# Second linear layer's q inside the second pass, grad_out by tiles, weight flips elsewhere, dWo of the last layer from on-chip o

## The chip, the cores and the metric

The kernel runs on one core of a Trainium2 chip. The time is that of one execution on the device in microseconds (us); the figure compared is the median over several runs. Times inside an execution come from one profiled execution.

## The reference

Four layers on x [1, 2048, 640] in bf16 with 32 heads of 20, alternating linear attention (A) and sliding-window attention of 256 (B), and the whole backward pass:

```python
def _A_ref(x, wqkv, wo):
    ...
    phi = lambda t: jnp.where(t > 0, t + 1, jnp.exp(t)) + 1e-6
    pq, pk = phi(q), phi(k)
    kv = jnp.einsum("bhsd,bhse->bhde", pk, v)
    z = jnp.einsum("bhsd->bhd", pk)
    num = jnp.einsum("bhqd,bhde->bhqe", pq, kv)
    den = jnp.einsum("bhqd,bhd->bhq", pq, z)[..., None] + 1e-6
    o = num / den
    ...
# _B_ref: softmax(q k^T / sqrt(20)) over the last 256 positions, times v
x = A_x
x = x + _A_ref(_layernorm(x, axis=-1), A_wqkv, A_wo)
x = x + _B_ref(_layernorm(x, axis=-1), B_wqkv, B_wo)
x = x + _A_ref(_layernorm(x, axis=-1), A_wqkv, A_wo)
x = x + _B_ref(_layernorm(x, axis=-1), B_wqkv, B_wo)
# returned: x and, from grad_out, the gradients of A_x, A_wqkv, A_wo, B_wqkv, B_wo
```

## The kernel before

The layers are numbered 0 (A), 1 (B), 2 (A), 3 (B). The 2048 positions are 16 tiles of 128. A "flip" is a transpose done by DMA, always issued from SP (line 404); plain DMAs go through SP or ACT (line 400).

`forward` goes through the tiles in two passes. `ab_pass(0)` does for each tile the numerator and division of layer 0 (`a_num`; its matmuls are at lines 624 and 432), the output projection, LN and qkv of layer 1 (`out_proj`, `ln`, `b_qkv`), the sliding attention (`attn`: scores at line 764, exponentials at 768 and 771, values at 802) and its output projection, and, two tiles behind, LN, k and v of layer 2 (`a_first`). Layer 2's q is not computed there: its normed input stays, flipped, in pqT, in the place of the q to come. `ab_pass(2)` then does the same for layers 2 and 3, and beside it, by `dO_steps`, the gradient dO of layer 3's attention output (grad_out tile flipped, times Wo_B flipped), with the sums that the softmax gradient needs.

Between the passes stand `late_q` for all 16 tiles (q of layer 2: ten matmuls at line 534, exponential at 538, minimum at 540, sum at 542, flip back into pqT, stores of pq and eq), `a_kv(2)` (the kv sums over all tiles, mbd), and `early_dO` (grad_out loaded in two halves over pk, Wo_B flipped into WoTB).

Buffers are rings, used in the order of the program. Those that matter here: s1, two PSUM tiles for the fourth head of a score group, which late_q uses as well; mm, two PSUM tiles (mm_ps) through which all projections, numerators and dO go; e, four buffers e_sb for score exponentials; ee and pp for exponentials and q; wT, one buffer through which `wflips` turns 35 pieces of 160 KB of the weights for the backward pass (15 of Wqkv_B, 15 of Wqkv_A, 5 of Wo_A), flip in and store out, spread over the second pass; o3, two buffers for the o of layer 3, which is stored to DRAM. Many small buffers of the second pass lie over vv, the v of layer 2, which is dead after a_kv(2).

The order is written by a list planner (`Sched`): each piece of work has a place in the pass (`AT`: tile number plus an offset, in tiles), and from these and assumed durations and dependencies (with some that only keep order, such as `after_kv`) it fixes the order on each of the five queues. TensorE's work may run ahead of that order by at most AHEAD places; work marked filler is outside that limit. Hardware waits come from the buffers themselves. Each queue runs in its fixed order, so an instruction that waits holds up what follows.

After the forward pass, `bwd_phase(None, None, 3)` computes dWo of layer 3 (o transposed times grad_out, 160 matmuls at line 1014), loading o back column by column (om, from SP), with nine loads and flips of the first slabs for the attention backward in between (`attn_slabs`, lines 326 and 1440). Then `B_attn_bwd(3)` runs (first scores at line 1496), then the backward of layers 2 and 1 and 0, which the change does not touch.

## Time and profile before

| what | value |
|---|---|
| median of 3 runs | 2291.28 us (2289.39 to 2301.68) |
| profiled execution | 2304.79 us, span 2303.1 us |
| mean granted TensorE clock | 0.960 |
| TensorE, VectorE, ScalarE, GpSimd busy | 88%, 63%, 52%, 38% |
| DMA | 376.80 MB, mean 164 GB/s |
| first numerator, first score of the second pass | 454.62, 506.74 us |
| last projection of the forward pass, first scores of the attention backward | 759.28, 804.74 us |

The span runs from the first to the last instruction of the profiled execution; the execution's own time is 1.7 us longer. In what follows PE is TensorE, PEld its weight loads, DVE VectorE, ACT ScalarE, POOL GpSimd, SP SyncE; SPq and ACTq are DMA issues on these queues. The ends of matmuls are modelled by the profile.

### The profile page before, as it was taken

The numbers are of one execution on the slowest core, as the hardware profiler recorded it, in microseconds if no ns is written. First come the engines' busy times: TensorE is split into PE (matmuls) and PEld (weight loads), VectorE is DVE, ScalarE is ACT, GpSimd is POOL, SyncE is SP. The second block draws the span as 40 slices with busy tenths as digits, with TensorE's granted clock in tenths as the row PEclk, the third lists the DMA queues.
The fourth block names the chain that finished last, engine by engine and source line by source line (L and its number), as shares of the span: only waits on it lengthen the run. The fifth ranks groups of instructions, "written<-read, shape, count | busy, mean of one in ns | idle before, by whom it ended". The sixth has DMA issues, their size and how long they took to land. (4 is left out here: it accounts for less than half of the span.)

```text
span 2303.1 us, 68489 instructions
## 1 busy us (share of the span) xinstructions
PE 2030.2 (88%) x28066; PEld 1418.4 (62%) x28066; DVE 1454.3 (63%) x2994; ACT 1196.8 (52%) x1981; POOL 878.8 (38%) x1850
## 2 busy tenths in 40 slices
PE   6879998779998689999899989998999988997899
PEld 4646666546665367777656567656777775654664
DVE  6657776567675189999734349605989983443551
ACT  4527777327777188888522223215888871110330
POOL 1016666206777155555322213203555551220110
PEclk9979999899999789999999999998999999998999
DMA  7428887589998757776877789935767768878973
GB/s 257 163 97 182 177 188 174 172 216 214 216 221 190 166 108 135 124 132 128 174 163 162 183 167 207 184 100 126 126 132 124 134 138 170 189 161 195 194 152 101
DMA packets 944763, 376.80 MB, mean 164 GB/s; under 512 B 822720, under 2 KB 924736, under 8 KB 944192
## 3 DMA queue, kind: packets, MB, share of 16 engines
q1 hardware_dynamic: 862288, 295.75, 63.7%
q10 hardware_dynamic: 82160, 76.68, 10.9%
q8 instruction: 219, 3.59, 0.7%
q14 instruction: 96, 0.79, 0.1%
HBM read 111.64 MB, written 114.95 MB: 98 GB/s over the span
## 5 line engine op out<-in xcount | busy, mean ns | idle before, releaser
L1531 DVE TENSOR_TENSOR ds_sb<-pair,e_sb 128x768 bf16<-128x768 f32 x480 | 436.3, 948 | 45.1 <-POOL e_sb L1520 45.0
L1516 ACT ACTIVATE e_sb<-pair 128x768 bf16<-128x768 f32 x480 | 388.9, 812 | 113.4 <-PE pair L1496 107.7
L777 POOL TENSOR_SCALAR_AFFINE_SELECT e_sb<-e_sb 128x384 bf16<-128x384 bf16 (+1 forms) x512 | 197.8, 406 | 396.6 <-ACT e_sb L768 363.0
L768 ACT ACTIVATE e_sb<-s_ps 128x1152 bf16<-128x1152 f32 (+2 forms) x256 | 273.5, 1068 | 112.5 <-PE s_ps L764 71.3
L1014 PEld LDWEIGHTS <-om 128*128 128x128 bf16 x1920 | 193.7, 101 | 195.1 <-DMA om<-o 31.7
L1014 PE MATMUL mm_ps<-wq,dqT 128*128 128x320 bf16 x1920 | 283.7, 303 | 25.2 <-DMA dqT<-dqkv 25.1
L1523 POOL TENSOR_SCALAR_AFFINE_SELECT e_sb<-e_sb 128x256 bf16<-128x256 bf16 x448 | 182.1, 406 | 266.0 <-ACT e_sb L1516 257.4
L1014 PE MATMUL mm_ps<-dqkv,om 128*128 128x480 bf16 x1280 | 273.8, 373 | 0.0
L1185 POOL TENSOR_TENSOR gw<-w,gcar 128x640 f32<-128x640 f32 x64 | 89.4, 1397 | 483.0 <-ACT w L1182 473.5
L1520 POOL TENSOR_SCALAR_AFFINE_SELECT e_sb<-e_sb 128x256 bf16<-128x256 bf16 x512 | 206.5, 406 | 115.0 <-ACT e_sb L1516 113.6
L1014 PEld LDWEIGHTS <-dqT 128*128 128x128 bf16 x1920 | 185.1, 99 | 103.0 <-DMA dqT<-dqkv 29.3
L1167 ACT ACTIVATE dh<-mm_ps 128x320 f32<-128x320 f32 x128 | 56.0, 437 | 331.4 <-PE mm_ps L1014 289.6
L1544 PE MATMUL dsT_ps<-ident,ds_sb 128*128 128x128 bf16 x2244 | 193.4, 224 | 28.7 <-ACT dsT L1548 25.1
L1548 ACT COPY dsT<-dsT_ps 128x768 bf16<-128x768 bf16 x240 | 190.9, 795 | 12.4 <-PE dsT_ps L1544 6.4
L1544 PEld LDWEIGHTS <-ds_sb 128*128 128x128 bf16 x2244 | 140.3, 99 | 92.2 <-issue 88.7
L1560 PE MATMUL dqvk_ps<-Ksl,dsT 128*128 128x32 bf16 x2160 | 167.5, 178 | 3.8 <-DVE dqkv L1569 3.0
L1560 PEld LDWEIGHTS <-dsT 128*128 128x128 bf16 x2880 | 156.2, 97 | 22.8 <-issue 21.7
L432 PE MATMUL mm_ps<-Wqkv_B,hnTB 128*128 128x320 bf16 x960 | 166.3, 305 | 3.0 <-DVE qk_slab L673 1.6
L1564 PE MATMUL dqvk_ps<-dOsl,e_sb 128*128 128x32 bf16 x2160 | 165.2, 177 | 0.0
L1564 PE MATMUL dqvk_ps<-Qsl,ds_sb 128*128 128x32 bf16 x2160 | 165.2, 177 | 0.0
L1496 PE MATMUL pair<-KTg,QTg 32*128 32x384 bf16 (+2 forms) x768 | 122.5, 322 | 25.8 <-DVE ds_sb L1531 24.2
L1564 PEld LDWEIGHTS <-ds_sb 128*128 128x128 bf16 x2880 | 144.9, 96 | 0.0
(189 smaller groups left out, 3913.4 us busy)
## 6 DMA issues: line engine op xcount, KB each, us to landing
qkvp<-qk_slab SPq DMA_DIRECT2D x64, 256.0 KB, 3.0
om<-o SPq DMA_DIRECT2D x20, 512.0 KB, 4.6
hn<-hn SPq DMA_DIRECT2D x64, 160.0 KB, 3.1
om<-hn SPq DMA_DIRECT2D x20, 512.0 KB, 4.8
qkvp<-v_slab SPq DMA_DIRECT2D x32, 256.0 KB, 2.6
o<-o SPq DMA_DIRECT2D x48, 160.0 KB, 3.2
Ksl<-qkvp SPq DMA_DIRECT2D x12, 512.0 KB, 4.5
Qsl<-qkvp SPq DMA_DIRECT2D x12, 512.0 KB, 4.3
```

Of the source, the lines that this page charges most:

```text
L432: nc.tensor.matmul(ps.t[:, w0:w0 + width], lhsT=lhsT(), rhs=rhs(), start=start, stop=stop)
L768: op("ACT", av(3 * nkt * P), lambda: nc.scalar.activation(e.t[:, 0:3, 0:nkt, :], s3.t[:, :, 0:nkt * P].rearrange("p h (i q) -> p h i q", q=P),
L777: nc.gpsimd.affine_select(out=v, in_=v, compare_op=ALU.is_ge, fill=0.0, base=0, pattern=[[0, h1 - h0], [1, P]], channel_multiplier=-1)
L1014: nc.tensor.matmul(ps.t[:, w0:w0 + width], lhsT=lhsT(), rhs=rhs(), start=start, stop=stop)
L1516: nc.scalar.activation(e, PR[h][:, :, 0:3 * P].rearrange("p i (j q) -> p i j q", q=P), ACT.Exp, scale=self.c_att)
L1520: nc.gpsimd.affine_select(out=e[:, :, j, :], in_=e[:, :, j, :], compare_op=ALU.is_ge, fill=0.0, base=0, pattern=[[0, 2], [-1, P]], channel ...
L1523: nc.gpsimd.affine_select(out=e[:, :, j, :], in_=e[:, :, j, :], compare_op=ALU.is_ge, fill=0.0, base=-1, pattern=[[0, 2], [1, P]], channel ...
L1531: nc.vector.tensor_mul(DS[n][:, hs], PR.pop(h)[:, :, 0:3 * P].rearrange("p i (j q) -> p i j q", q=P), E[n][:, hs])
L1544: nc.tensor.transpose(ps[:, i, j, :], DS[n][:, 2 * p + i, j, :], self.ident)
L1548: (nc.vector.tensor_copy if h % 2 else nc.scalar.copy)(TSB[h], TPS.pop(h))
L1560: nc.tensor.matmul(a[:, 0, hh, :], lhsT=TSB[2 * n + hh // 2][:, hh % 2, j, :], rhs=ld[g]["K"][:, k, cs], start=(i == 0), stop=(i == len(dq ...
L1564: nc.tensor.matmul(a[:, 1 + x, hh, :], lhsT=src[n][:, hh, j, :], rhs=ld[g][rhs][:, q, cs], start=(i == 0), stop=(i == len(dkv) - 1))
```

## The change

late_q of tiles 4 to 15 moves into the second pass, 3.225 tiles ahead of each tile, with its PSUM from mm instead of s1 and no longer as filler; four stay between the passes. grad_out is loaded tile by tile in the second pass. Wo_B's flips into WoTB come after the first LN of layer 3. The 15 flips of Wqkv_B come between the passes, through the four e buffers; the 20 of Wqkv_A and Wo_A come in the first pass, through pp, from place 1.644 at a quarter of a tile each. The o of layer 3 gets 16 buffers: 11 over the k and v columns of Wqkv_A and a spare slice behind it, two over vv, the last three over its q columns. Neither this o nor its linv is stored. dWo of layer 3 is computed from it at the end of the forward pass; `bwd_phase(None, None, 3)` goes, and the slab loads follow the forward pass on SP directly. AHEAD becomes 13, and the times in AT change a little. The diff, with context cut:

```diff
@@ -19,7 +19,7 @@
 LN_EPS = 1e-5
-AHEAD = 12
+AHEAD = 13
 IDLE = 300
@@ -361,7 +361,7 @@
-                wT=ring("wT", 1, [P, DT, P]), rt=ring("rt", 2, [P, H], F32), li=ring("li", 2, [P, H], F32),
+                rt=ring("rt", 2, [P, H], F32), li=ring("li", 2, [P, H], F32),
@@ -373,23 +373,30 @@
             WoTB = over_vv(DT * D).rearrange("p (k n) -> p k n", k=DT)
-            R["o3"] = Ring(2, tiles=[over_vv(D) for _ in range(2)], name="o3")
             R["gT"] = Ring(2, tiles=[over_vv(D).rearrange("p (k q) -> p k q", k=DT) for _ in range(2)], name="gT")
             R["dd"] = Ring(2, tiles=[over_vv(2 * H).bitcast(F32) for _ in range(2)], name="dd")
+            R["res"] = Ring(2, tiles=[over_vv(CW) for _ in range(2)], name="res")
             pqT = big.tile([P, DT, T], BF, name="pqT")
+            qks = [big.tile([P, DP], BF, name=f"qk_slab{i}") for i in range(3)]
+            vs = [big.tile([P, H, HPAD], BF, name=f"v_slab{i}") for i in range(5)]
+            R["qk"], R["v"] = Ring(3, tiles=qks), Ring(5, tiles=vs)
+            wsb = {k: big.tile([P, DT, n], BF, name=k) for k, n in (("Wqkv_B", QT), ("Wo_A", D))}
             mbd = big.tile([P, DT, D + P], BF, name="mbd")
             zcol = big.tile([P, DT], F32, name="zcol")
-            qks = [big.tile([P, DP], BF, name=f"qk_slab{i}") for i in range(3)]
-            vs = [big.tile([P, H, HPAD], BF, name=f"v_slab{i}") for i in range(5)]
-            R["qk"], R["v"] = Ring(3, tiles=qks), Ring(5, tiles=vs)
+            space = big.tile([P, TT * D], BF, name="Wqkv_A")
+            assert TT * D >= DT * QT
+            wsb["Wqkv_A"] = space[:, 0:DT * QT].rearrange("p (k n) -> p k n", k=DT)
+            own = [space[:, i * D:(i + 1) * D] for i in range(TT)]
+            free = [own[i] for i in range(TT) if i % 3 or i >= 3 * DT] + [over_vv(D) for _ in range(2)]
+            n_free = len(free)
+            R["o3"] = Ring(TT, tiles=(free + own[0::3])[:TT], name="o3")
+            wsb["Wo_B"] = big.tile([P, DT, D], BF, name="Wo_B")
...
-            wsb = {k: big.tile([P, DT, n], BF, name=k) for k, n in
-                   (("Wqkv_B", QT), ("Wqkv_A", QT), ("Wo_A", D), ("Wo_B", D))}
             S = Sched(tc, ahead=AHEAD)
@@ -521,13 +528,16 @@
-            def late_q(l, tt):
-
-                sv, F = self.sv[l], dict(filler=True)
+            q_left = set(range(TT))
+
+            def late_q(l, tt, where="s1", **F):
+
+                sv = self.sv[l]
+                q_left.discard(tt)
                 e, p_ = R["ee"].buf(), R["pp"].buf()
                 for ci in range(2):
-                    ps, c0 = R["s1"].buf(), ci * CW
+                    ps, c0 = R[where].buf(), ci * CW
                     for k0, k1 in ((0, 2), (2, DT)):
@@ -690,22 +700,39 @@
             def early_dO():
-                for l in (0, 1):
-                    dma("ACT", lambda l=l: g[:, 8 * l:8 * l + 8, :],
-                        lambda l=l: self.tm_view(self.grad_out)[:, 8 * l:8 * l + 8, :], 1280 * KB,
-                        [], [("g", tt) for tt in range(8 * l, 8 * l + 8)])
-                    after_kv(S.ops[-1])
                 for et in range(DT):
                     flip(lambda et=et: WoTB[:, :, et * P:(et + 1) * P], lambda et=et: wsb["Wo_B"][:, et, :], 160 * KB,
-                         ["Wo_B"], ["WoTB"])
+                         ["Wo_B", ("rs", 3, 0)], [("WoTB", et)])
                     after_kv(S.ops[-1])
-                dma("SP", lambda: W["WoTB"].rearrange("p (a b) -> p a b", a=DT), lambda: WoTB, 800 * KB, ["WoTB"], [])
+                dma("SP", lambda: W["WoTB"].rearrange("p (a b) -> p a b", a=DT), lambda: WoTB, 800 * KB,
+                    [("WoTB", et) for et in range(DT)], [])
                 for t in dslabs:
+            def early_dWo():
+                for m in range(DT):
+                    for ci in range(2):
+                        ps, res, c0 = R["mm"].buf(), R["res"].buf(), ci * CW
+                        for t0, t1 in ((0, 5), (5, 10), (10, TT - 1), (TT - 1, TT)):
+                            def f(ps=ps, m=m, c0=c0, t0=t0, t1=t1):
+                                for tt in range(t0, t1):
+                                    nc.tensor.matmul(ps.t[:, 0:CW], lhsT=att_out[3, tt][0].t[:, m * P:(m + 1) * P],
+                                                     rhs=g[:, tt, c0:c0 + CW], start=(tt == 0), stop=(tt == TT - 1))
+                            op("PE", pe([CW] * (t1 - t0)), f, [("g", tt) for tt in range(t0, t1)] +
+                               [(att_out[3, tt][0], q) for tt in range(t0, t1) for q in (0, 1)], [ps])
+                        op("ACT", av(CW), lambda ps=ps, res=res: nc.scalar.copy(res.t, ps.t[:, 0:CW]), [ps], [res])
+                        after_kv(S.ops[-1])
+                        dma("ACT", lambda m=m, c0=c0: self.dWoB_part[m * P:(m + 1) * P, c0:c0 + CW], lambda res=res: res.t,
+                            2 * P * CW, [res], [])
+
             def dO_steps(tt):
                 c = {}
+
+                def load_g():
+                    dma("ACT", lambda: g[:, tt, :], lambda: self.tm_view(self.grad_out)[:, tt, :], 160 * KB,
+                        [("rs", 3, max(tt - 1, 0))], [("g", tt)])
+                    after_kv(S.ops[-1])
@@ -743,7 +770,7 @@
                     return f
-                return turn_g, chunk(0), chunk(1)
+                return load_g, turn_g, chunk(0), chunk(1)
@@ -812,10 +839,15 @@
                             if l == 3:
+                                assert b < n_free or q_left == set()
                                 after_kv(S.ops[-1])
+                                S.ops[-1].deps.update(o_ for i in range(6) for o_ in S.rd.get(("Wqkv_A", i), ())
+                                                      if b >= n_free or o_ in a_users)
                         if g == G - 1 and p_ == 1:
                             turn("mm" if b >= TT - 2 else None, lambda: oT.t, lambda: o.t, DT, ks, [oT])
+                            if l == 3:
+                                return
                             dma("ACT", lambda: self.tm_view(self.sv[l]["o"])[:, b, :], lambda: o.t, 160 * KB, ks, [])
@@ -834,18 +866,22 @@
-            def wflips(tag, i):
+            def wflips(tag, i, where, gate):
                 def f():
                     c0 = part * D if part < 3 else 0
-                    b = R["wT"].buf()
+                    b = R[where].buf()
+
+                    def bt():
+                        v = b.t if where == "pp" else b.t.rearrange("p a b q -> p (a b q)")[:, 0:D]
+                        return v.rearrange("p (k q) -> p k q", k=DT)
                     keys = [("Wqkv_A", i) for i in range(6)] if key == "Wqkv_A" else [key]
-                    keys = keys + [("rs", 2, TT - 1)]
-                    flip(lambda: b.t, lambda: wsb[key][:, et, c0:c0 + D], 160 * KB, keys, [b])
+                    keys = keys + [gate]
+                    flip(bt, lambda: wsb[key][:, et, c0:c0 + D], 160 * KB, keys, [b])
                     dma("SP", lambda: W[dst].rearrange("p (a b) -> p a b", a=n)[:, a:a + DT, et * P:(et + 1) * P],
-                        lambda: b.t, 160 * KB, [b], [])
+                        bt, 160 * KB, [b], [])
                 return f
@@ -875,8 +911,9 @@
-            AT = {0: dict(num=-2.454, out=-1.75, outb=1.744, step=0.167, qkv=-0.991, wide=0.77, lag=0.288, af=2.09, al=0.036),
-                  2: dict(num=-2.43, out=-1.76, outb=1.696, step=0.077, qkv=-1.035, wide=0.611, lag=0.314, gT=0.12, dO=1.593, dOs=0.1)}
+            EARLY = 4
+            AT = {0: dict(wf=1.644, num=-2.454, out=-1.75, outb=1.703, step=0.148, qkv=-0.99, wide=0.759, lag=0.332, af=2.09, al=0.036),
+                  2: dict(lq=-3.225, num=-2.43, out=-1.76, outb=1.696, step=0.059, qkv=-0.894, wide=0.584, lag=0.314, gT=-0.208, dO=1.691, dOs=0.1)}
@@ -938,12 +975,16 @@
                 if last:
-                    spread(items, 2.0, 13.0, [wflips(t, i) for t in "BA" for i in range(4 * DT) if t == "A" or i % 4 < 3])
+                    for tt in range(EARLY, TT):
+                        items.append((tt + a["lq"], len(items), lambda tt=tt: late_q(l, tt, "mm")))
+                    items.append((0.01, len(items), early_dO))
                     for tt in range(TT):
-                        for at, f in zip((a["gT"], a["dO"], a["dO"] + a["dOs"]), dO_steps(tt)):
+                        for at, f in zip((a["gT"] - 0.5, a["gT"], a["dO"], a["dO"] + a["dOs"]), dO_steps(tt)):
                             items.append((tt + at, len(items), f))
                     a_first(items, l + 2, a["af"], a["al"], range(TT))
+                    for i in range(4 * DT):
+                        items.append((a["wf"] + 0.25 * i, len(items), wflips("A", i, "pp", ("rs", 1, 0))))
                 run(items)
@@ -956,13 +997,16 @@
             ab_pass(0, False)
-            for tt in range(TT):
-                late_q(2, tt)
+            for tt in range(EARLY):
+                late_q(2, tt, filler=True)
+            for i in range(3 * DT):
+                wflips("B", 4 * (i // 3) + i % 3, "e", ("rs", 2, TT - 1))()
             a_kv(2)
                         for o in S.rd.get(k, ())}
-            early_dO()
+            a_users = {o for i in range(6) for o in S.rd.get(("Wqkv_A", i), ())}
             ab_pass(2, True)
+            early_dWo()
             nc.scalar.preload_act_table_set("natural_log_exp_and_others")
@@ -1634,8 +1678,9 @@
             early = self.attn_slabs(3, 0, slab0, L)
-            whens = [1.0, 2.0, 3.0, 4.0, 5.0, 6.0, 7.0, 8.0, 9.0]
-            self.bwd_phase(None, None, 3, [(w, *e) for w, e in zip(whens, early)])
+            with self.tc.manual_schedule(engines={mybir.EngineType.SP}):
+                for _, _, _, f in early:
+                    f()
             self.B_attn_bwd(3, self.dqkv, slab0, L)
             raw = p_.tile([P, 7 * self.T], BF, name="slabA")
```

More of the change, by code (lines that the diff above doesn't have):

```diff
@@ L722, in f @@
                         mm_chunk(ps, CW, [(lambda k=k: b.t[:, k, :], lambda k=k: WoTB[:, k, c0:c0 + CW],
-                                           k == 0, k == DT - 1) for k in range(DT)], [b, "WoTB"])
+                                           k == 0, k == DT - 1) for k in range(DT)], [b] + [("WoTB", et) for et in range(DT)])
                         op("DVE", vp(CW), lambda: nc.vector.tensor_tensor(
```

## Prediction

> **What bounds the kernel now.** I read the page first. TensorE is busy for 88% of the span and no other engine's share comes near:
>
> ```profile
> PE 2030.2 (88%) x28066; PEld 1418.4 (62%) x28066; DVE 1454.3 (63%) x2994; ACT 1196.8 (52%) x1981; POOL 878.8 (38%) x1850
> ```
>
> Time is to be had where TensorE stands still. The change touches the first 805 us alone, so I cut these by stages with the table of windows (columns: window, its length, then busy time of PE, PEld, DVE, ACT, POOL, granted clock, DMA share, GB/s).
>
> ```profile
> core 0: us, PE busy (x) PEld busy (x) DVE busy (x) ACT busy (x) POOL busy (x), PEclk, DMA share, GB/s
> 210.00:390.00 180.00, 167.36 (x2832) 118.79 (x2831) 131.59 (x329) 140.58 (x230) 115.02 (x251) 1.00 0.82 180
> 439.00:507.00 68.00, 43.94 (x307) 27.39 (x306) 39.07 (x109) 13.71 (x34) 0.00 (x0) 0.85 0.93 247
> 540.00:720.00 180.00, 167.08 (x2964) 115.11 (x2961) 126.58 (x305) 139.50 (x204) 137.48 (x282) 1.00 1.08 217
> 720.00:761.00 41.00, 30.95 (x544) 21.26 (x544) 18.38 (x41) 27.21 (x36) 29.25 (x61) 0.83 0.62 145
> 761.00:805.00 44.00, 26.51 (x170) 17.33 (x171) 3.94 (x10) 4.25 (x10) 0.40 (x1) 0.81 0.85 186
> ```
>
> The two steady passes (first and third row) keep TensorE busy for 93% of the time at full clock; work added there costs nearly its own length. Two stretches are loose: between the passes (second row: 44 of 68 us busy, at clock 0.85), and after the second pass, where dWo of layer 3 runs (last row: 26.5 of 44).
>
> The timeline of TensorE (start, us, instruction, and the idle time before it with what ended it) shows what fills the first, and so does one row of its table of waits (who waited for whom: us in total, times, longest).
>
> ```profile
> 454.62 0.32 PE L432 MATMUL mm_ps<-mbd,pqT 128*128 128x32 bf16 x5 [6.63 <-DMA pqT<-pp]
> ...
> 505.29 1.52 PE L534 MATMUL s_ps<-Wqkv_A,pqT 128*128 128x320 bf16 x10 [1.20 <-DVE pp L542]
> 506.74 0.23 PE L764 MATMUL s_ps<-QT,KT 32*128 32x128 bf16 x3
> ```
> ```profile
> PE s_ps L534 <- DVE pp L542: 16.3, 12, 2.5
> ```
>
> Line 534 is late_q. Sixteen of them pass through the two s1 PSUM tiles, and attention (line 764) draws from the same ring, so its first score stands behind the last late_q, at 506.74, though the first numerator of the pass was already multiplied at 454.62. Near the end the PE does ten matmuls, waits 1.2 us for VectorE, and does ten more.
>
> The second stretch, and what the weight DMAs and slab loads do in it:
>
> ```profile
> 759.28 1.58 PE L432 MATMUL mm_ps<-Wo_B,oTB 128*128 128x320 bf16 x10
> 762.89 0.34 ACTq L400 DMA_DIRECT2D dOpt<-vv  x1
> 766.36 10.28 PE L1014 MATMUL mm_ps<-gcar,om 128*128 128x320 bf16 x64 [5.49 <-DMA om<-o]
> 781.27 1.48 SPq L326 DMA_TRANSPOSE dOTg<-dOpt  x1
> 787.87 11.45 PE L1014 MATMUL mm_ps<-gcar,om 128*128 128x320 bf16 x64 [11.23 <-DMA om<-o]
> 799.70 4.52 PE L1014 MATMUL mm_ps<-gcar,om 128*128 128x320 bf16 x32 [0.39 <-DMA om<-o]
> 804.74 0.50 PE L1496 MATMUL pair<-KTg,QTg 32*128 32x128 bf16 x10 [0.51 <-ACT res L1102]
> ```
>
> dWo's 160 matmuls take 10.28 + 11.45 + 4.52 = 26.2 us; the rest of the 44 us is waiting for om, the o of layer 3 read back from DRAM, whose loads share SP with nine slab loads. The attention backward (line 1496) starts when dWo ends.
>
> **Part by part: between the passes.** Twelve of the sixteen late_q go, and the two bulk loads of grad_out, 2.5 MB. The first pass shows how the same code starts without late_q: from its first numerator to the flip of its first oTB.
>
> ```profile
> 123.39 0.72 PE L432 MATMUL mm_ps<-mbd,pqT 128*128 128x32 bf16 x5 [1.04 <-DVE mbd L598]
> 144.41 0.23 PE L764 MATMUL s_ps<-QT,KT 32*128 32x128 bf16 x4
> 170.83 1.25 SPq L404 DMA_TRANSPOSE oTB<-oB  x1
> ...
> 393.11 1.22 SPq L404 DMA_TRANSPOSE oTB<-oB  x1
> 521.66 1.32 SPq L404 DMA_TRANSPOSE oTB<-vv  x1
> ...
> 727.24 2.64 SPq L404 DMA_TRANSPOSE oTB<-vv  x1
> ```
>
> There it is 170.83 - 123.39 = 47.4 us (21.0 of it to the first score), here 521.66 - 454.62 = 67.0 us. I put the 47.4 in its place: 19.6 us less. It is not the 36 us by which the first score could move, because while late_q held attention back, the PE also did the numerators, output projections and qkv of the tiles to come; the first pass pays for these after its first score.
>
> The first numerator itself may come earlier. It waits for the flip of the first late_q, whose input was ready early (second row; the first is the last LN of the first pass, the others two flips of Wqkv_B through the one buffer wT):
>
> ```profile
> 429.11 0.45 PE L448 MATMUL mm_ps<-ident,hnA 128*128 128x128 bf16 x5
> ...
> 440.79 0.49 DVE L542 SCALAR_TENSOR_TENSOR pp<-s_ps,ee 128x320 bf16<-128x320 f32 x1
> ...
> 461.00 1.21 SPq L404 DMA_TRANSPOSE wT<-Wqkv_B  x1
> 471.22 1.23 SPq L404 DMA_TRANSPOSE wT<-Wqkv_B  x1
> ```
>
> Ready at 441.3, landed at 454.6: 13 us in a queue filled by grad_out, mbd and weight flips. grad_out leaves; fifteen flips of Wqkv_B with their stores are now bunched here, through four e_sb buffers. One buffer turned round in 471.22 - 461.00 = 10.2 us, so four of them pass a flip every 2.6 us, 38 us in all; in that time SP also has to slip in the four pqT flips, and a store that waits for its flip holds up what stands behind it on SP. I take 4.4 us for the earlier numerator, between 9 less and 6 more (one flip and its store ahead of each of three). Attention can take its first e_sb buffers when twelve of the fifteen are stored, 12 x 2.6 = 31 us after that LN at 429, so at 460; the first score, 21 us after a numerator at 450, needs them at 471. This is the cover, 11 us wide; the rival below is what it costs when it is gone. Sum of the part: -24 us, bounds -29 and -14.
>
> **The second pass.** Its tiles gain what left. One late_q:
>
> ```profile
> L534 PE MATMUL s_ps<-Wqkv_A,pqT 128*128 128x320 bf16 x160 | 30.4, 332 | 16.4 <-DVE pp L542 16.3
> L538 ACT ACTIVATE ee<-s_ps 128x320 bf16<-128x320 f32 x32 | 13.9, 437 | 57.7 <-PE s_ps L534 37.4 <-issue 5.5 <-DMA pq<-pp 3.9
> L542 DVE SCALAR_TENSOR_TENSOR pp<-s_ps,ee 128x320 bf16<-128x320 f32 x32 | 15.1, 487 | 5.9 <-DMA pqT<-pp 5.4
> ```
>
> Ten matmuls at the 0.141 us of the last 32 above (4.52 / 32) are 1.4 us; ACT gets 0.87 us, DVE 0.97 and two small minima. ACT stands at 77% and DVE at 70% in the third row of the windows, so the PE pays: 12 x 1.4 / 0.93 = 18 us if it keeps its busy share, 4 us if it spent its idle 7% of each tile on them. The first pass gives a second way: there two k and two v chunks a tile make the same ten matmuls more, out of the same two mm_ps buffers, and from first to fourteenth oTB it takes 393.11 - 170.83 = 222.3 us against 727.24 - 521.66 = 205.6, 16.7 us more. I take +17, bounds +10 and +21. SP loses twenty flips of Wqkv_A and Wo_A and gains twelve of pqT; ACT's queue loses the stores of o and linv of layer 3 and gains sixteen grad_out tiles and the pq and eq stores. No gain from that:
>
> ```profile
> PE mm_ps L432 <- DMA oTA<-oA: 1.9, 3, 1.1
> SPq L404 <- DVE oB L810: 64.3, 11, 6.9
> PE mm_ps L432 <- DVE gcar L504: 1.8, 8, 0.2
> ```
>
> The first row is all that the PE lost to oTA flips in 540 to 720; there is little for a lighter queue to give back. The new AT times and AHEAD 13 reorder this work without adding any; I count them as 0, plus or minus 3.
>
> **The first pass** gets the twenty flips and their stores, four a tile over some five tiles. On SP each is 1.25 us and about 0.5 for the store, 7 us a tile; the second row just above (210 to 390) shows SP idle for 64.3 us in ten tiles at one wait alone, 6.4 a tile. That leaves 0.6 us a tile uncovered: +3 us, bounds 0 and +15 (a rival below).
>
> **After the pass.** dWo no longer reads DRAM. But it takes its PSUM from the two mm_ps tiles in order, so its first matmul still follows the last output projection (ends 760.9, and some 0.5 us for its eviction); it fills no hole in the last tile. Then 160 matmuls: 22.6 us at the rate of the last 32, 25.7 at that of the first 64 (10.28 / 64 = 0.161), which began after a 5.5 us gap. I take 24, then 1 us for the copy that frees PSUM: first score at 786.5 instead of 804.7, -18 us, bounds -21 and -14. The Trainium skill (TensorE: Matmul & The Clock Gate, Part 1) says that the array starts at half clock after an idle window and reaches full clock after about 3.4 us of sustained work; by that rule, an estimate, this part would be about -18.5, and the windows' 0.83 and 0.81 agree that these stretches are partly cold. The slab loads are covered: dO of the last tile left at 762.89, and 781.27 is only the time at which SP got round to flipping it; ahead of SP now lie no om loads, so I expect it by 768 and landed by 773, 13 us before it is needed.
>
> **Sum:** -24 + 17 + 3 - 18 = -22 us, from 2304.8 us of the profiled execution (span 2303.1) to 2282.8. That execution was 13.5 us above the median of the runs, 2291.28; I carry the difference over: **2269 us**. The bounds of the parts, not all at one end, give 2257 to 2281 for this case.
>
> **Rivals.** *More hidden than I think*: the numerator comes at once (-29), late_q falls into the PE's gaps (+10), tail -20, first pass 0: -39, 2252. For it: every late_q has 0.8 of a tile before its numerator. Against: PE at 93%.
>
> *The weight flips hold attention back.* If four flips in flight slow each other, so that a buffer turns in 22 us rather than 10.2, twelve take 66 us from 429 and attention gets its buffers at 495, 24 us after it needs them; the gain between the passes is gone: 2293. It decides from a turn of 14 us (twelve flips in 42 us, from 429 to 471). For it: DMA share 0.93 there already. Against: grad_out's 2.5 MB leave.
>
> *DMA is full in the first pass.* Twenty flips and twenty stores of 160 KB are 6.6 MB in 87 us, 75 GB/s on top of 180 (first window row); the second pass got 217. If that is the ceiling, 87 us stretch by 255/217, 15 us instead of 3: 2281. The Trainium skill (DMA: Bandwidth & Descriptors, Issuing engines are not separate DMA queues) has all queues share the same 16 DMA engines, which speaks for this rival: moved traffic is not saved traffic. Against it in the rows: 247 GB/s between the passes, and at 217 the PE still lost only 1.9 us.
>
> *Slower: late_q starves the mm_ps ring.* A chunk of late_q leaves PSUM by ACT and then DVE, and ACT may be in a score exponential:
>
> ```profile
> L768 ACT ACTIVATE e_sb<-s_ps 128x1152 bf16<-128x1152 f32 x224 | 252.7, 1128 | 73.7 <-PE s_ps L764 35.8 <-DVE qk_slab L673 11.3 <-DVE vv L810 6.0
> ```
>
> With 1.13 us of waiting and 0.44 of its own, twice a tile, twelve tiles: up to 38 us more than in my sum, 2307. It decides from 2.8 us a tile (22 us of gain and 11.5 of measurement, over twelve), a tile of 20 us in place of the 17.1 of my sum. Against: the k chunks of the first pass leave the same two buffers in the same way, and cost the PE 1.8 us at line 504 in 180 us; its tile is 17.1.
>
> **Chances.** Forecast 0.56, more hidden 0.14, flips hold attention 0.10, DMA full 0.10, ring starved 0.10. A measurement of this kernel can tell about 0.5%, 11.5 us, from no change, so faster means below 2279.8: 0.53 of the forecast, the 0.14 and 0.04 of DMA full, 0.71. The same: the rest of the forecast (0.03), 0.06 of DMA full, the flips: 0.19. Slower: 0.10. The range leaves out the starved ring and the outer part of "more hidden": 2251 to 2293; the forecast's own is 2257 to 2281.
>
> **What would show it.** Right: the first score of the second pass 20 to 25 us after its first numerator; 12 late_q in mm_ps among the second pass, whose first to fourteenth oTB takes 220 to 225 us; no om load before the attention backward and its first score 24 to 27 us after the last output projection. Wrong: e_sb waiting for a weight store; SP late for QT or KT in the first pass; TensorE waiting on pp or ee in mm_ps for over 1 us a tile; dWo matmuls with gaps for res.

## The result and the profile after

The changed kernel takes 2272.93 us (median of five runs, 2270.36 to 2275.09); the ratio to before is 0.9909, 95% interval 0.9884 to 0.9933. Run again unedited beside other kernels it gave 0.9906 (0.9885 to 0.9928). 2269 us had been forecast, in a range of 2251 to 2293. The time is right; two of the four terms behind it are not, and their errors offset.

TensorE's busy time has hardly moved on the page of after, and it should not have: the change moves work, and the span loses idle time.

```profile
PE 2020.9 (89%) x28066; PEld 1415.0 (62%) x28066; DVE 1452.7 (64%) x2990; ACT 1195.5 (53%) x1981; POOL 883.0 (39%) x1850
```

The table of windows of after, cut at the same stages (columns as in the prediction):

```profile
225.00:405.00 180.00, 162.93 (x2709) 113.41 (x2711) 125.94 (x315) 133.16 (x220) 109.49 (x239) 0.98 0.84 178
451.00:489.00 38.00, 22.69 (x163) 13.79 (x161) 21.48 (x58) 4.28 (x12) 0.78 (x2) 0.78 1.03 228
530.00:710.00 180.00, 175.94 (x3007) 119.43 (x3005) 137.20 (x337) 144.70 (x220) 135.88 (x278) 1.00 0.95 208
711.00:752.00 41.00, 31.06 (x556) 21.48 (x549) 18.47 (x39) 27.42 (x37) 29.20 (x60) 0.83 0.34 87
752.00:775.00 23.00, 22.68 (x167) 16.14 (x166) 2.58 (x7) 4.12 (x10) 1.34 (x1) 1.00 0.64 147
```

Three rows differ in kind from before. The second pass (third row) keeps TensorE busy for 97.7% of the time, where it had been 93%. dWo (last row) runs without a gap and at full clock. And the first pass (first row) got looser: 162.9 of 180 busy, 167.4 before.

The next two fences are the tables of the tile oTB (transposes on SP's queue: count, shortest, median and longest ns, first and last start; of the second pass the o tiles lie in the memory named Wqkv_A or vv) and TensorE's timeline. They give the stages' lengths.

```profile
L411 SPq DMA_TRANSPOSE oTB<-oB x14: 1218/1461/2228, 169.8 to 407.6; - x14
L411 SPq DMA_TRANSPOSE oTB<-Wqkv_A x12: 1227/1284/2482, 509.4 to 719.2; - x12
```
```profile
463.32 0.32 PE L439 MATMUL mm_ps<-mbd,pqT 128*128 128x32 bf16 x5 [6.09 <-DMA pqT<-pp]
...
487.31 0.23 PE L791 MATMUL s_ps<-QT,KT 32*128 32x128 bf16 x4
...
749.73 2.48 PE L439 MATMUL mm_ps<-Wo_B,oTB 128*128 128x320 bf16 x10
...
752.79 1.65 PE L720 MATMUL mm_ps<-gcar,Wqkv_A 128*128 128x320 bf16 x11
...
774.11 0.57 PE L720 MATMUL mm_ps<-gcar,Wqkv_A 128*128 128x320 bf16 x3
775.19 0.50 PE L1540 MATMUL pair<-KTg,QTg 32*128 32x128 bf16 x10 [0.51 <-ACT vv L724]
779.45 0.51 PE L1540 MATMUL pair<-VTg,dOTg 32*128 32x128 bf16 x8 [3.75 <-DMA dOTg<-dOpt]
```

First to fourteenth oTB takes 237.9 us in the first pass (222.3 before) and 209.8 in the second (205.6). From the fourteenth flip to the next first numerator it is 55.7 us (61.5 before), from that numerator to the first oTB of the second pass 46.1 (67.0), the first score coming 24.0 us after the numerator. The end of the tail is best read where the attention backward has its first complete block, at its first dqvk matmul (tables of the tiles Wo_B and dqvk_ps, first of before, then of after):

```profile
L432 PE MATMUL mm_ps<-Wo_B,oTB x160: 296/299/310, 529.1 to 760.6; 128*128 128x320 bf16 x160
L1560 PE MATMUL dqvk_ps<-Ksl,dsT x368: 175/177/234, 814.9 to 899.2; 128*128 128x32 bf16 x184
```
```profile
L439 PE MATMUL mm_ps<-Wo_B,oTB x160: 296/299/474, 514.8 to 751.9; 128*128 128x320 bf16 x160
L1604 PE MATMUL dqvk_ps<-Ksl,dsT x492: 176/176/234, 788.2 to 899.1; 128*128 128x32 bf16 x164
```

From the last output projection that is 54.3 us before and 36.3 after. At that matmul after is 26.7 us ahead; the parts are +15.6 and -5.8 in and behind the first pass, -20.9, +4.2, -18.0, and -1.8 in the pieces between. The whole spans differ by 31.9 us, but the profiled execution of before was a long one; the ratio says about 21. Behind that matmul no run changes anything, and still that stretch takes between 1475.6 and 1492.8 us in the fourteen profiles (1488.2 in before, 1483.0 in after), so whole spans of single profiles are not compared below.

### The profile page after: what moved, and what is told of

Its sections match the earlier page's. It is cut to its first block, busy times and chain, and to the rows that moved or that the text cites. A ratio compares the mean times of both kernels' runs of the same rounds, so it can differ in the third digit from the quotient of the medians.

```text
span 2271.2 us, 68393 instructions
## 1 busy us (share of the span) xinstructions
PE 2020.9 (89%) x28066; PEld 1415.0 (62%) x28066; DVE 1452.7 (64%) x2990; ACT 1195.5 (53%) x1981; POOL 883.0 (39%) x1850
## 5 line engine op out<-in xcount | busy, mean ns | idle before, releaser
L1058 PEld LDWEIGHTS <-om 128*128 128x128 bf16 x1760 | 176.1, 100 | 165.4 <-DMA om<-o 13.0
L1592 ACT COPY dsT<-dsT_ps 128x768 bf16<-128x768 bf16 x240 | 191.0, 796 | 11.6 <-PE dsT_ps L1588 5.3
```

The lines of the kernel that those rows point to most:

```text
L1058: nc.tensor.matmul(ps.t[:, w0:w0 + width], lhsT=lhsT(), rhs=rhs(), start=start, stop=stop)
L1592: (nc.vector.tensor_copy if h % 2 else nc.scalar.copy)(TSB[h], TPS.pop(h))
```

## The experiments

Ratios compare each kernel with runs of before made beside it. The stages, read in each profile from the same rows as above, in us ("num to oTB" is from the first numerator of the second pass to its first oTB, "tail" from the last output projection to the first dqvk matmul):

| kernel | first pass | num to oTB | second pass | tail | ratio, 95% interval |
|---|---|---|---|---|---|
| before | 222.3 | 67.0 | 205.6 | 54.3 | 1 |
| after | 237.9 | 46.1 | 209.8 | 36.3 | 0.9909 (0.9884 to 0.9933) |
| after_again | 238.4 | 47.4 | 209.4 | 36.0 | 0.9906 (0.9885 to 0.9928) |
| retune_alone | 229.9 | 66.9 | 206.2 | 55.1 | 1.0058 (1.0037 to 1.0079) |
| at0_undone | 226.5 | 46.3 | 208.1 | 35.3 | 0.9884 (0.9858 to 0.9909) |
| ahead12 | 229.1 | 45.8 | 210.0 | 35.8 | 0.9865 (0.9845 to 0.9885) |
| flips_wide | 235.9 | 47.2 | 210.1 | 36.4 | 0.9914 (0.9886 to 0.9942) |
| early16 | 233.7 | 76.6 | 202.0 | 35.5 | 0.9998 (0.9982 to 1.0014) |
| q_mm_twice | 234.2 | 47.9 | 224.3 | 36.4 | 0.9974 (0.9957 to 0.9990) |
| b_flips_pass2 | 238.8 | 42.7 | 230.8 | 36.4 | 0.9953 (0.9937 to 0.9969) |
| one_store | 234.1 | 47.7 | 209.9 | 33.4 | 0.9895 (0.9869 to 0.9921) |
| dwo_late | 236.0 | 45.1 | 210.0 | 57.3 | 0.9994 (0.9978 to 1.0010) |
| best1 | 227.0 | 46.3 | 209.9 | 33.4 | 0.9845 (0.9822 to 0.9869) |
| best2 | 222.8 | 46.1 | 208.2 | 33.2 | 0.9864 (0.9848 to 0.9881) |

### The first pass: weight flips or the new order?

Four edits ask what the 15.6 us are. **retune_alone**, on before:

```diff
-AHEAD = 12
+AHEAD = 13
-  0: dict(num=-2.454, ..., outb=1.744, step=0.167, qkv=-0.991, wide=0.77, lag=0.288, ...)
+  0: dict(num=-2.454, ..., outb=1.703, step=0.148, qkv=-0.99, wide=0.759, lag=0.332, ...)
```

> Before with only the first pass's due times and AHEAD 13 of after; no weight flip in the first pass, everything else as before. Theory 'the due times cost half of the first pass's loss': a_kv ends at about 444 to 445 instead of 438.55, and the time rises by about 6 us, ratio 1.002 to 1.004. Rival 'the flips cost all of it': a_kv ends at 438 to 440, ratio 0.999 to 1.001.

**at0_undone** is the same edit backwards, on after:

> After with the first pass's due times (outb, step, qkv, wide, lag) and AHEAD 12 of before; the 20 weight flips stay in the first pass. Theory 'the due times cost half of the first pass's loss': the end of the a_kv matmuls comes 6 to 7 us earlier than in after (451.3), at about 445, with the gain in tiles 4 to 13 (163.2 us back to about 157), and the kernel takes about 2266 us, ratio 0.988. Rival 'the flips cost all of it': the first pass keeps its 12 to 13 us, a_kv ends at 450 to 452, ratio 0.990 to 0.992. Second rival, that the new due times were what held the loss down: a_kv ends after 453 and the ratio is over 0.993.

**ahead12**, on after, goes back to `AHEAD = 12` and nothing else:

> After with AHEAD 12 and all due times of after. Both together cost 7.6 us of the first pass without flips (229.9 against 222.3) and about 9 with them (235.8 on average against 226.5 and 227.0). If AHEAD, the number of places by which an instruction of TensorE may be drawn forward in the order, is what costs: first pass 225 to 229 us, 8 us under after_again. If the due times cost: 233 to 239 us and the time of after_again within 4 us.

**flips_wide**, on after:

```diff
-                        items.append((a["wf"] + 0.25 * i, len(items), wflips("A", i, "pp", ("rs", 1, 0))))
+                        items.append((a["wf"] + 0.65 * i, len(items), wflips("A", i, "pp", ("rs", 1, 0))))
```

> The 20 weight flips of the first pass are due every 0.65 tile (13 tiles) instead of every 0.25 (5 tiles). Theory 'each flip takes transfer time wherever it lies, and the due times cost the rest': tiles 1 to 4 fall from 58.1 us to about 53, tiles 4 to 13 rise by 3 to 5 us, the pass ends within 2 us of after's (a_kv end 449 to 453), ratio 0.990 to 0.992. Rival 'crowding': only the dense stretch, where the DMA share is 1.0, costs anything; spread out, the flips are covered, a_kv ends 5 to 7 us earlier (about 445) and the ratio is about 0.988.

**after_again** gives the spread:

> The changed kernel once more, unedited, beside the three others on their chip: how far the same code moves from one profiled execution to the next. The five edits of it that left its first pass as it was took 233.7 to 238.8 us from first to fourteenth oTB of that pass (237.9 in the profile of after); if that spread is the executions' own, this one lies in it too, and the second pass at 209 to 211 us, ratio 0.988 to 0.993.

Seven profiles have exactly the first pass of after: after, after_again, one_store, early16, q_mm_twice, b_flips_pass2 and dwo_late. They take 233.7 to 238.8 us, 236.2 on average. So one profile tells some 5 us here and no less. The tables of the tile oTB, in the order retune_alone, at0_undone, ahead12, flips_wide:

```profile
L404 SPq DMA_TRANSPOSE oTB<-oB x14: 1231/1486/2792, 169.2 to 399.1; - x14
```
```profile
L411 SPq DMA_TRANSPOSE oTB<-oB x14: 1222/1249/2554, 169.5 to 396.0; - x14
```
```profile
L411 SPq DMA_TRANSPOSE oTB<-oB x14: 1205/1402/2284, 172.8 to 401.9; - x14
```
```profile
L411 SPq DMA_TRANSPOSE oTB<-oB x14: 1227/1398/2602, 168.4 to 404.3; - x14
```

The new order costs 229.9 - 222.3 = 7.6 us without a single flip, and undoing it in after gives 236.2 - 226.5 = 9.7 back. AHEAD alone gives 236.2 - 229.1 = 7.1 of them, by one profile, and its ratio lies below after_again's, the two intervals meeting at 0.9885. The flips are the rest: 226.5 - 222.3 = 4.2 us for twenty in the old order, 236.2 - 229.9 = 6.3 in the new one. Alone the 4.2 would be within the spread of single profiles; best1 and best2 below differ by 4.2 again. flips_wide takes 235.9, the average of the seven, so spreading the flips over the pass gains nothing that can be seen. In time retune_alone missed upward, 1.0058 where 1.002 to 1.004 was expected, which is 13 us; its profile shows 7.2 us up to the first dqvk matmul, and the other 6 stay open: behind that matmul its profile is shorter than that of before, 1475.6 us against 1488.2. The steady part, from the windows of after and of ahead12:

```profile
210.00:390.00 180.00, 162.07 (x2701) 113.05 (x2700) 126.50 (x316) 132.33 (x218) 108.95 (x238) 0.98 0.88 181
```
```profile
210.00:390.00 180.00, 164.38 (x2749) 115.39 (x2747) 127.98 (x324) 134.27 (x222) 110.80 (x242) 0.99 0.89 188
```

With AHEAD 13 TensorE is busy for 2.3 us less in these 180 and does 48 matmuls fewer; the transfers' share is about the same. The two kernels differ in the order of the instructions alone, so the order is what costs, without any work added. None of TensorE's waits carries it. A wait of ACT changes with the due times, its exponentials behind the flip of oTB, which they don't read (ACT's table of waits, 170 to 405 us, of after and then of at0_undone):

```profile
ACT e_sb L798 <- DMA oTB<-oB: 9.3, 4, 2.7
```
```profile
ACT e_sb L798 <- DMA oTB<-oB: 1.8, 1, 1.8
```

It is 8.6 to 13.9 us in the ten profiles with the new due times (8.6 in ahead12), 1.8 to 3.6 in the three with the old, and absent in before. As ahead12 has it too, it is no effect of AHEAD, and it is not shown to cost the pass anything; which pair of instructions is now the wrong way round stays open.

### The second pass: what does late_q cost?

**early16**, on after, sets `EARLY = 16`: all sixteen late_q before the pass.

> All sixteen late_q between the passes (EARLY 16), none in the second pass; the rest as after, so no weight flip and no bulk load of grad_out in the second pass. Theory 'the flips held the gaps': the second pass lost its idle 7% to its 35 weight flips, and late_q cost its full length; then without either, first to fourteenth oTB of the second pass takes about 195 us (209.8 in after, 205.6 in before). Theory 'late_q fills the gaps': the gaps stay open without late_q, and it takes 204 to 207 us. In both the stretch from first numerator to first oTB grows again from 46.1 us by 17 to 21, to 63 to 67. The time: about 2276 us by the first theory (ratio 0.993), about 2286 by the second (0.997). The forecast's own terms (+17 in the pass, -19.6 between the passes) say about no difference from after.

**q_mm_twice**, on after:

```diff
-                            for k in range(k0, k1):
+                            for k in (list(range(DT)) if where == "mm" and k0 == 0 else []) + list(range(k0, k1)):
                                 nc.tensor.matmul(ps.t[:, 0:CW], lhsT=own()[:, k, :], ..., start=(k == 0), stop=(k == DT - 1))
-                        op("PE", pe([CW] * (k1 - k0)), f, ...)
+                        op("PE", pe([CW] * (k1 - k0 + (DT if where == "mm" and k0 == 0 else 0))), f, ...)
```

The second pair of lines tells the planner the longer duration.

> In each of the twelve late_q of the second pass the five matmuls of each half are done once more, ahead of the real ones, into the same PSUM tile that the real ones then start afresh: 120 matmuls, 16.9 us of TensorE at 0.141 us, and nothing else on any engine. The second pass of after has 2.3% of TensorE idle time left, 4.8 us in 210. Theory: the gaps are used up, so the second dozen costs its length: first to fourteenth oTB 223 to 227 us, the kernel 15 to 17 us over after, ratio 0.997 to 0.999. Rival: the pass is set by ACT or by the attention chain, and TensorE's share of 98% is only waiting that the trace counts as busy; then the pass grows by less than 8 us, ratio under 0.995.

**b_flips_pass2**, on after:

```diff
-            for i in range(3 * DT):
-                wflips("B", 4 * (i // 3) + i % 3, "e", ("rs", 2, TT - 1))()
...
+                    spread(items, 2.0, 13.0, [wflips("B", 4 * (i // 3) + i % 3, "pp", ("rs", 2, TT - 1)) for i in range(3 * DT)])
```

> The 15 flips of Wqkv_B go back from the stretch between the passes into the second pass, spread over 11 tiles and through the two pp buffers; else as after. Theory 'flips cost their share of transfer time in either pass': at the 4.5 us that 20 flips seem to cost in the first pass (a_kv results 441.9 with them, 437.4 without, same due times), 15 cost 3 to 4 us of the second pass (213 us from first to fourteenth oTB), and the stretch between the passes gives back less than 2, so 1 to 4 us slower than after, ratio 0.991 to 0.993. Rival 'flips held 10 us of gaps in the second pass of before': 15 of 35 bring back 4 to 6 us, over 214 us. Second rival: the flips are covered, and the stretch between the passes gains by their leaving (numerator before 460, first oTB under 44 us after it): 3 to 6 us faster, ratio under 0.989.

For each of the three, in this order, the table of the tile oTB and then the windows:

```profile
L411 SPq DMA_TRANSPOSE oTB<-Wqkv_A x12: 1200/1234/1243, 537.4 to 739.4; - x12
```
```profile
545.00:725.00 180.00, 170.52 (x3017) 119.92 (x3016) 131.65 (x312) 141.26 (x206) 138.21 (x286) 1.00 0.93 190
```
```profile
L411 SPq DMA_TRANSPOSE oTB<-Wqkv_A x12: 1212/1236/2648, 511.0 to 735.3; - x12
```
```profile
530.00:710.00 180.00, 177.88 (x2911) 121.87 (x2908) 127.65 (x318) 135.49 (x206) 125.03 (x257) 1.00 0.91 194
```
```profile
L411 SPq DMA_TRANSPOSE oTB<-Wqkv_A x12: 1222/1350/2045, 506.7 to 737.5; - x12
```
```profile
530.00:710.00 180.00, 160.63 (x2740) 112.81 (x2737) 123.97 (x309) 131.81 (x201) 123.94 (x253) 1.00 1.03 216
```

Without flips and without late_q the pass takes 202.0 us, between the two theories (195, and 204 to 207). So both hold in part. early16 and after differ in EARLY alone: the twelve late_q cost 7.8 us (202.0 to 209.8), not their full 17, since TensorE's idle 5.3% of the empty pass (170.5 of 180) went down to 2.3%. The other 3.6 us (205.6 to 202.0) are what the leaving of 35 flips and their stores is worth together with all else that changed in this pass: no stores of o and linv, grad_out by tiles, new due times. The second dozen has nothing left to fill: 14.5 us for 120 matmuls of 16.9, as expected within 3 us. early16's ratio missed both theories' 0.993 and 0.997: before the pass the stretch grew by 29 to 31 us, not by 17 to 21, and the kernel is as slow as before.

The flips of b_flips_pass2 were a plain miss: 21 us for fifteen, where twenty cost 4.2 in the first pass. That is one profile, 16.8 us behind after at the first dqvk matmul; the ratios have 0.9953 against 0.9909, some 10 us. Between the passes their leaving gave back 3.4 us (46.1 to 42.7), where less than 2 was expected. TensorE is busy for 160.6 of 180, and its wait for score exponentials (510 to 735 us) grew from 5.0 us in after to 13.2. Part of the cause shows in ACT's table of waits, 510 to 735 us, and at its longest wait in ACT's timeline:

```profile
ACT e_sb L795 <- DMA hnTB<-hnB: 4.4, 1, 4.4
...
ACT e_sb L795 <- DMA WqTB<-pp: 2.1, 1, 2.1
ACT e_sb L795 <- DMA KT<-qk_slab: 1.6, 1, 1.6
```
```profile
602.61 0.48 ACT L798 ACTIVATE e_sb<-s_ps 128x384 bf16<-128x384 f32 x1
607.02 0.33 ACTq L407 DMA_DIRECT2D o<-oA  x1
607.45 1.13 ACT L795 ACTIVATE e_sb<-s_ps 128x1152 bf16<-128x1152 f32 x1 [4.35 <-DMA hnTB<-hnB]
```

An exponential reads none of these. ACT stood at a store of its own queue, in order, behind somebody else's transfer: the store of o shares a completion counter with SP's flip of hnTB, which landed at 606.94. The next experiment shows the same for SP. The three rows are 8.1 us of ACT. Counted transfer by transfer in the trace, twelve of ACT's in this pass start within 0.1 us of the landing of the earlier one on their counter, after 15.1 us of idle ACT in all; in after there is one, with 0.3. The flips also share their two pp buffers with late_q here; no run separated the two, so the counters are argued as the larger part, not shown.

### The tail: what holds the slab loads?

In SP's timeline of after the slab loads start late, although SP has nothing to do for 34 us:

```profile
726.44 1.23 SPq L411 DMA_TRANSPOSE vv<-gcar  x1
761.56 1.27 SPq L326 DMA_TRANSPOSE QTg<-qkvp  x1
...
774.52 2.45 SPq L326 DMA_TRANSPOSE dOTg<-dOpt  x1
```

**one_store**, on after: the results of dWo go to the memory of WoTB, whose last reader is done, and leave in one transfer.

```diff
-                        op("ACT", av(CW), lambda ps=ps, res=res: nc.scalar.copy(res.t, ps.t[:, 0:CW]), [ps], [res])
-                        dma("ACT", lambda m=m, c0=c0: self.dWoB_part[m * P:(m + 1) * P, c0:c0 + CW], lambda res=res: res.t,
-                            2 * P * CW, [res], [])
+                        op("ACT", av(CW), lambda ps=ps, m=m, c0=c0: nc.scalar.copy(WoTB[:, m, c0:c0 + CW], ps.t[:, 0:CW]), ...)
+                dma("ACT", lambda: self.dWoB_part.rearrange("(m p) n -> p m n", p=P), lambda: WoTB, 800 * KB, ...)
```

> The ten result copies of the early dWo go into the memory of WoTB, and one 800 KB store is issued after the last of them, instead of ten stores of 80 KB between the copies. Theory 'queued behind the stores': in the profile of after each slab load is issued only when a dWo store four to eight transfers earlier in the program has landed (QTg at 761.56 right after the third store, KTg at 765.16 after the fourth, and so on to dOTg at 774.52), so with one store behind them no slab load waits for a dWo store: QTg should be issued some 20 us before the last dWo matmul, dOTg before the first score, the stall of 3.75 us ahead of the first VTg,dOTg matmul should go, and the time should fall by 3 to 4 us, to a ratio of about 0.989 to before (0.9909 with the ten stores). Rival 'queues full or data late': the slab loads are late because their own source rows (the last qkvp or dOpt stores) land late; then QTg is still issued after 758 and the stall keeps at least 3 us.

SP's timeline and the longest of its waits in one_store:

```profile
727.22 1.27 SPq L326 DMA_TRANSPOSE QTg<-qkvp  x1
...
751.81 1.17 SPq L326 DMA_TRANSPOSE dOTg<-dOpt  x1
...
776.12 1.16 SPq L326 DMA_TRANSPOSE dOTg<-dOpt  x1
```
```profile
SPq L326 <- DMA dWoB_part<-vv: 19.9, 1, 19.9
SPq L1485 <- DMA dOpt<-vv: 8.0, 2, 5.2
SPq L326 <- DMA out_dram<-x: 6.0, 1, 6.0
```

QTg leaves 34 us earlier, the first dOTg 23, and TensorE's 3.75 us wait for dOTg is gone. Only one load still waits for a store of dWo, the second half of dOTg. In the trace the transfers of SP and ACT signal eight completion counters in turn, and each starts only when the earlier one on its counter, eight places ahead in program order, has landed. In after that is the third of the ten stores for QTg: it landed at 761.54, and QTg started at 761.56. In one_store it is the one store for the second dOTg: landed at 776.10, started at 776.12. The other loads now stand in the same way behind the last stores of dO and x (the two lower rows), early enough to cost nothing here. None of the loads reads what the store of dWo writes. The tail is 33.4 us, 2.9 less (3 to 4 expected); eight profiles with the ten stores have 35.3 to 36.4, the three with the one store 33.2 to 33.4. The ratio, 0.9895, agrees but can't show it.

**dwo_late**, on after: no early_dWo, o of layer 3 stored again, dWo in the phase that before has for it.

> After with the tail of before: o of layer 3 is stored and read back, dWo runs in its own phase with the nine slab loads among its loads, and no early dWo. Theory of the tail, -18 forecast and -16.3 read in the two profiles: from last output projection to the first dqvk matmul again 53 to 56 us instead of 36.3, the kernel 16 to 20 us over after_again, ratio 0.996 to 1.000. Rival: the earlier start of dWo was mostly taken back later (slab loads of the second head group in the way); then under 10 us over after_again.

```profile
L439 PE MATMUL mm_ps<-Wo_B,oTB x160: 296/299/474, 511.7 to 750.2; 128*128 128x320 bf16 x160
...
L1601 PE MATMUL dqvk_ps<-Ksl,dsT x402: 176/176/234, 807.5 to 899.7; 128*128 128x32 bf16 x134
```

The tail is 57.3 us (53 to 56 expected), 21 more than in after, and the ratio rises from 0.9906 to 0.9994, 20 us. By the ratio the whole net gain of the change is this part, and the other three add up to about nothing: 1 us, with an interval from 5 us of gain to 2 of loss. The single profiles leave more to them, as dwo_late is 7.4 us ahead of before at the first dqvk matmul (807.5 against 814.9).

### Two kernels that beat after

**best1** joins at0_undone and one_store:

> After with both edits that gained: AHEAD 12 and the first pass's due times of before, and the one store of dWo. If they add: a_kv's results at 440 to 444, no stall ahead of the first VTg,dOTg matmul, 5 to 7 plus 3 to 4 us under after, about 2263 us, ratio 0.986 to 0.988. If the slab loads, now issued from 720 on, hold up transfers of the last tiles, the second gain is lost and the ratio stays at 0.988 to 0.990.

**best2** moves the twenty flips of the first pass to the first stage as well:

```diff
-                    for i in range(4 * DT):
-                        items.append((a["wf"] + 0.25 * i, len(items), wflips("A", i, "pp", ("rs", 1, 0))))
...
+            for i in range(4 * DT):
+                items.append((6.0 + 0.45 * i, len(items), wflips("A", i, "e", ("rs", 0, 5))))
             run(items)
             a_kv(0)
```

> best1 (AHEAD 12 and the due times of before in the first pass, one store for dWo) with the 20 flips of Wqkv_A and Wo_A moved out of the first pass into the first stage (20 to 120 us, DMA share 0.5, SP idle for most of it), through the four e_sb buffers that nothing uses there. Theory 'flips cost 4 to 5 us in the pass and nothing where transfers are idle': first pass back to 221 to 224 us from 227.0, the first stage not over 1 us longer, 4 us under best1, ratio 0.981 to 0.984. Rival: the 4.4 us were not the flips', first pass 226 to 228 and the ratio of best1, 0.9845. Second rival, the flips delay the first stage by their own length, as SP also carries hn and the weight loads: num of the first pass 5 us later, no gain.

best1 has the lowest ratio, 0.9845 (2264.02 us), where 0.986 to 0.988 was expected; its interval overlaps those of ahead12 and best2. In its profile the two gains stand side by side, 227.0 us in the first pass and 33.4 in the tail. The first pass of best2 is at 222.8, so 4.2 us less, as the theory of the flips' price has it; but the windows of the first stage show where they went (best1, then best2):

```profile
20.00:120.00 100.00, 84.11 (x701) 59.27 (x702) 64.15 (x183) 54.38 (x132) 0.00 (x0) 0.93 0.50 178
```
```profile
20.00:120.00 100.00, 78.42 (x667) 55.81 (x667) 59.48 (x171) 50.18 (x124) 0.00 (x0) 0.93 0.88 234
```

TensorE loses 5.7 of 84.1 us in a stage with half of the transfer time free, and the first numerator of that pass comes at 132.2 instead of 127.1: the second rival. In the twelve other profiles, whose first stage has no flips either, it comes at 120.6 to 124.0, so the flips cost that stage 5 us by this pair and 8 to 12 by the others. The two ratios can't be told apart.

## Why the prediction was right, point by point

**Between the passes (-24 forecast).** Right in size: -20.9 from numerator to first oTB, -19.6 forecast, and the first score 24.0 us after the numerator (20 to 25); the numerator came 5.8 us sooner behind the first pass's last flip (4.4). What it is made of was not seen: early16 keeps all sixteen late_q and takes 76.6 us, so the twelve are worth 30 us, and some 10 of these are given back (76.6 against the 67.0 of before). The bunched flips of Wqkv_B are a part of that: without them, in b_flips_pass2, the stretch is 3.4 us shorter. The rest stays open. The proxy from the first pass hit the net, in part by luck, as it has no such flips.

**The second pass (+17 forecast, +4.2 measured, under its bound of +10).** It takes 209.8 us, where 220 to 225 was the sign of being right. The step that failed is "the PE pays: 18 us if it keeps its busy share", and the first-pass proxy taken to confirm it. The other end that was written there, 4 us if late_q goes into the idle 7%, is nearer: late_q costs 7.8. "No gain from that", said of the lighter queues, was wrong too: the pass without late_q is 3.6 us under before, from the flips that left or from what changed with them. The waits of TensorE on transfers, 1.9 us, had seemed to bound it.

**The first pass (+3 forecast, +15.6 in the profile, 13.9 by the average of the seven).** The flips' own term was nearly right, 4.2 to 6.3. "I count them as 0, plus or minus 3", said of AHEAD and the due times, is the failed step: 7 to 10 us. The text looked for work that was added, and an order costs without any.

**The tail (-18 forecast, -18.0 measured)**, but not by its steps. dWo took 21.9 us (752.79 to the last matmuls from 774.11), not 24, at clock 1.00: the last projections ahead of it had paid for the cold start, with 0.56 of the clock granted from 745 to 752.5. The Trainium skill (TensorE: Matmul & The Clock Gate, Part 1) has the array at full clock after a window of sustained work and at half clock after an idle one. For dWo, right behind busy TensorE, the trace agrees; for the projections it agrees less, as TensorE's gaps ahead of them, from 725 us on, are 1.3 us at most. The first score came 25.5 us after the last projection's row (24 to 27), which is 20.0 less than before (45.5); some 3 of these were lost again on the way to the first dqvk matmul. But "the slab loads are covered, landed by 773" failed: dOTg was issued at 774.52 and TensorE stood 3.75 us. I had reckoned SP's queue free and forgot what a free queue can still wait for.

**The rivals.** "DMA is full in the first pass" put 2281 on a ceiling of 217 GB/s; over ten tiles the share is 0.84 at 178 GB/s, and ten of the fourteen lost microseconds go with AHEAD and the due times. Only between 180 and 240 us, with the flips under way, is the share at 1.0; their 4.2 us may be that. The Trainium skill (DMA: Bandwidth & Descriptors, Issuing engines are not separate DMA queues) has all transfers run on the same 16 engines. By that the first stage, with the share at 0.50, looked like the place for them; best2 shows that there, with the share at 0.88 after, TensorE pays no less. "The weight flips hold attention back" came in a small part: the first score stood 24.0 us behind the numerator instead of 21, and the 3.4 us of b_flips_pass2 are a seventh of that rival's 24. "More hidden than I think" had late_q at +10, nearer than the forecast, and the first pass at 0, further off. "late_q starves the mm_ps ring" did not come; the groups of after show 120 of its matmuls in mm_ps with no idle time before them:

```profile
L544 PE MATMUL mm_ps<-Wqkv_A,pqT 128*128 128x320 bf16 x120 | 18.7, 299 | 0.0
```

So the sum of -22 came out as -26.7 in the profiles: against the forecast's terms, 11 us were lost in and behind the first pass and 13 won in the second, and the small pieces won 3. That these offset is luck, and so is how close the time came; the median moved by 18.4.

## What to carry to other kernels

What moved work costs depends on what else is in its stage: price it by a run that leaves the stage without it, not by the busy share, which says how much room there is but not who fills it. A reordering in a change's diff is a term of the sum like any other, and the first to undo alone when a stage comes out longer. Before calling a load covered because its queue is empty, look which earlier transfers it must see landed, those of other queues too.

## What the runs showed of the hardware that was not expected

- Through the completion counters that this program's transfers share, a transfer on an idle queue stood up to 33.8 us (row of SP's waits in after, 730 to 800 us, below) behind stores of another engine's queue whose data it doesn't touch; with one store in place of ten it left at 727.22 instead of 761.56.

```profile
SPq L326 <- DMA dWoB_part<-vv: 39.0, 4, 33.8
```

- The price of a weight flip with its store differs by stage, in single profiles: 0.2 to 0.3 us each in the first pass (4.2 / 20 and 6.3 / 20), 1.4 in the second pass beside late_q (21 / 15), 0.3 to 0.6 in a stage with half of the transfer time free (5.1 / 20 to 11.6 / 20).
- One and the same first pass took 233.7 to 238.8 us in seven profiled executions.
